# Sliding-window attention on block-diagonal keys with stationary exponentials, its output turned by DMAs, under a new order

## The chip, the cores and the metric

The kernel runs on one core of a Trainium2 chip. The metric is the device time in microseconds of one execution; the kernel before has three such times. A profile is one further execution, recorded instruction by instruction. The engines are named as the profile names them: PE is TensorE (PEld its weight loads), DVE is VectorE, ACT is ScalarE, POOL is GpSimd and SP is the engine that mostly issues DMAs.

## What is computed

The reference normalises x (2048 tokens of width 448), runs a dilated sliding-window attention and a two-layer feed-forward on the normalised rows, and joins them. Cut to what matters:

```
xn = layernorm(x)                               # [2048, 448]
q, k, v = split(xn @ wqkv, heads=16, width=28)
idx = pos[:, None] - 2 * arange(8)              # 8 keys, every second one back
attn = softmax(where(idx >= 0, q . k[idx] / sqrt(28), -1e9))
s = (sum over the 8 of attn * v[idx]) @ wo
h = gelu(xn @ w1 + b1)                          # 448 -> 1792
g = silu(h @ w2 + b2)                           # 1792 -> 448
out = x + s * g
```

The kernel reorders tokens into even ones (first half of 2048 positions) and odd ones, so that the window is eight neighbouring positions. A block of 57 queries then needs 64 neighbouring keys.

## The kernel before

Work is cut into 16 tiles of 128 tokens (four chunks of four tiles) and, for the attention, nine blocks of four strips of 57 (or 56) queries.

**Stages.** `norm` normalises a tile (square root of the variance on ACT in `rstds` for the first four tiles, a power on POOL for the others) and turns it into `xnT`, by PE for the first four tiles and by a transposing DMA (`dma_T`) for the rest. `qk_rows` and `vproj` project to q, k and v; `qk_rows` ends in a transposing DMA that gives `qkT`, with 32 partitions per head in four groups. `values` copies 64 rows of v per strip from `v_tok` to `v`, from SBUF to SBUF on POOL's queue. `ff1`, `ff2_pair` and `ff2` are the feed-forward; `gate` its last function; `final_pair` and `final` multiply with `wo`, and `store` joins and writes out.

**Attention of a block** (`scores`, `values_sum`). The scores are 64 products per block, each with 32 rows of contraction, 64 stationary key columns and 57 query columns, spread over eight corners of the PE array, into four PSUM banks with keys on the partitions. ACT takes the exponential out of each bank (L660), DVE multiplies with the mask (L666). The sums over values are 64 products with v stationary (64 x 32) and the exponentials moving; a column of ones in v gives the softmax sum. Their result has features on the partitions and queries along the row. To divide, DVE transposes each of two banks by 32 x 32 blocks (L692), takes reciprocals (L696), spreads them back by another transpose (L701) and multiplies into `oT` (L706). `move` then repacks the fourth slab of `oT` through DRAM: one store and four loads for every two tiles, on SP.

**Pairs.** Most 448- and 512-column products run as pairs with 64 rows of contraction each, on the upper and the lower half of the array (`pair`). Between the two parts of a pair stands an instruction on POOL or SP that only waits (`told`, L424): PE's second part waits for it, so whatever that queue holds ahead of it delays PE.

**Order.** Each unit of work is a task with its dependencies and buffers. `ORDER` lists every task once, with a letter for its engine (P, V, A, G, S for PE, DVE, ACT, POOL, SP; D for a DMA's landing) and its number by creation. The instructions are emitted exactly in that order, and each engine runs its own in order. Buffers come from small pools (`p_b` has the eight PSUM banks); a task that takes a buffer waits for its last reader.

**Function tables.** ACT holds one table set at a time. Square root, tanh-form gelu, exponential (with tanh) and silu need four different ones; where the set in place is not the one that the next function needs, the built program has a table load ahead of it. Six small tasks made by `table` (L326 to L334) run one function each on a single column (`sink`): gelu, exp, gelu, exp, gelu, silu. In the order before they stand as A54 to A59 in six different places, the first behind the work of the first four tiles and the last near the end:

```
V22 S38 ... S42 D43 A53 G32 ... V61 V64 P9 A62 ... A152 A153 A54 S154
A534 A544 ... A545 A55 V355 ... A784 ... A786 A56 V758 ... A565 A57 ... A840 A58 ... A609 A59
```

Of the kernel before, what the change touches and what calls it, by code (L numbers as in the profile page):

```python
# [8 lines left out]
F32 = mybir.dt.float32  # L9
# [8 lines left out]
D0 V1 G17 S34 D35 A36 D37 V15 P2 V16 V22 S38 D39 V23 V24 G50 V25 V26 V27 P3 S44 D45 V28 V29 V30 G51 D52 V18 V19 P4  # L18
V20 S40 D41 V21 G31 P5 S42 D43 A53 G32 P6 G33 S46 D47 P7 V60 S48 D49 P8 V61 V64 P9 A62 S76 D77 G100 P10 V63 P11 P12
V106 S78 D79 P13 P14 V107 P108 S80 D81 V65 P109 A66 V110 A111 V67 P132 V113 D112 G102 G104 S82 D83 V114 P115 P136  # L20
V117 V68 S86 D87 P116 P133 A118 V69 P190 D119 P137 A70 V71 S88 D89 V120 P134 V121 V72 S90 D91 P122 P123 P135 V73
V191 V124 A74 P138 V75 D125 V126 P149 A139 V127 V140 A143 P128 G150 P129 A148 S141 D142 P151 A152 A153 A54 S154 D155
G178 D179 V130 V144 D131 P321 G174 D175 P326 P163 G327 G322 P323 G164 V96 V94 V95 G168 D169 V97 V92 V145 G99 V200
V204 A325 P328 P165 A166 V201 S202 D203 A330 V205 P341 G342 A324 A329 P336 A167 G337 V84 V85 V93 G98 V192 P343 P338
A339 A340 S206 D207 V105 P331 V193 S194 D195 V196 A344 V197 G332 P156 S198 D199 S274 D275 V309 G157 S272 D273 V298
S278 D279 V304 V305 G186 D187 P333 G188 D189 P158 P316 S146 D147 A335 V311 V312 S276 D277 V307 G317 P346 P318 A160
A159 P227 A345 G347 G184 D185 A319 A334 G228 V308 P348 A350 P229 P526 G527 P546 G252 D253 A320 G547 A349 P528 A529
V300 S161 D162 A530 P536 G537 A231 P548 A550 V310 P538 P516 G517 P215 G294 D295 A230 A549 P518 A519 G216 P222 G223
V103 A520 P217 V219 A539 G180 D181 P224 A540 V301 A225 A226 P521 P531 G522 P523 A525 G532 P533 A524 V218 G170 D171
S220 D221 P208 V302 A535 V303 V299 G306 V101 V359 P541 G209 P210 A211 V351 V363 V364 G542 P543 P621 V360 G172 D173  # L30
S361 D362 A534 A544 V313 V314 V352 G182 D183 P693 A545 A55 V355 V356 S357 D358 G176 D177 G315 V212 V439 A694 V695
A700 A696 V701 V697 G296 D297 G280 D281 A698 G622 S213 D214 P623 V627 G258 D259 P711 A718 A712 V624 A716 P241 S365
D366 V427 V428 A714 V699 A628 P234 V719 G242 P386 V435 G235 V713 S353 D354 V715 S429 D430 S387 G256 D257 P702 P236
V238 A237 P243 V245 P388 V389 A390 P630 G631 G246 D247 A244 G405 D406 S239 D240 A625 V436 V431 P729 S437 D438 G284
D285 P632 A734 V629 V703 V704 V717 V705 V706 A730 A736 P374 V440 S375 A732 V733 S441 D442 S232 D233 G292 D293 G250
D251 V737 P443 G444 V735 V633 G264 D265 G266 D267 G248 D249 P376 V731 P445 A447 A634 V626 G855 V378 P367 V707 A377
P720 V708 V636 A637 G368 V725 V432 A446 V709 V710 G254 D255 V721 P369 A371 S379 A370 D380 V726 V722 V723 V724 P639
S873 D874 V727 V728 P747 A748 A752 G290 D291 G268 D269 G409 D410 S433 D434 S372 D373 V638 A754 V635 G640 P641 V642
P400 G401 P393 V645 A646 V753 A750 P738 P402 S391 D392 V739 G260 D261 P381 A404 G382 V740 V403 S394 P395 A396 V741
V742 V397 G282 D283 P383 A384 G856 G270 D271 V743 V744 G488 D489 V745 V746 P457 S877 D878 G458 S883 D884 A385 P469  # L40
P459 A461 S470 P471 S867 D868 A460 A473 G262 D263 P476 V472 P765 A766 P450 G288 D289 G477 G415 D416 V751 A768 V749
S871 D872 G413 D414 G451 S861 D862 V755 A772 P478 A480 G419 D420 A770 V479 G286 D287 G407 D408 P452 V453 P756 S891
D892 S887 D888 P783 V761 V762 V757 A454 V647 A788 A784 V785 G490 D491 A790 S885 D886 G423 D424 A786 A56 V758 P648
S863 D864 S889 D890 G411 D412 V763 V764 V773 V767 V787 G417 D418 S857 D858 S398 D399 S875 D876 S859 D860 P462 V789
S869 D870 A643 V644 P581 S463 P464 A466 V769 S881 D882 G492 D493 S865 D866 V759 V465 G649 V760 S893 D894 P650 G582
P583 A585 P556 V651 A652 A584 P571 S557 P558 A559 G572 P573 P576 G425 D426 S897 D898 G421 D422 V654 V653 A655 V771
A575 V791 P774 A574 V775 V776 S879 D880 G498 D499 G500 D501 S577 V777 A560 P578 A580 G494 D495 S448 D449 P551 G552
G482 D483 S455 D456 A579 G504 D505 P566 P553 S899 D900 A555 S901 D902 P964 V779 V656 V780 G484 D485 V781 V782 G965
S567 P568 P966 G496 D497 A569 V778 A570 P953 G954 V967 P561 G562 V971 V968 P955 P563 P792 V972 G510 D511 S467 D468
V956 S903 D904 A554 V960 V961 S911 D912 V793 A564 S474 D475 S909 D910 V794 G486 D487 V797 V798 A565 A57 S895 D896  # L50
P801 A804 A802 A806 V795 V796 V803 S969 D970 V805 V807 P657 G658 P819 A822 G512 D513 S905 D906 V799 G502 D503 A820
V800 S913 D914 A808 V809 V957 P659 V663 V660 A664 G481 A824 S907 D908 V823 A826 P810 V815 S919 D920 S962 V811 D963
A661 P666 V816 P837 A842 V812 V817 S915 D916 V813 V818 V814 S973 D974 G667 P668 P975 S958 D959 A844 S923 D924 A838
P986 V843 S987 S921 D922 V662 V672 V665 S927 D928 P591 S929 D930 V669 G976 V825 S925 D926 P988 A840 A58 V827 P977
V989 V990 V982 G592 S931 D932 A673 V993 P593 A595 P586 V821 A594 S587 S991 D992 V674 S917 D918 V983 V978 V979 G506
D507 P596 P588 A590 A589 P828 G597 P598 A599 A600 V829 P616 V833 V830 V831 P611 V834 S612 V835 V836 G617 P618 G514
D515 G508 D509 A619 A620 V832 V845 A670 V994 V839 S984 D985 S933 D934 S941 D942 S935 D936 P1008 G1009 V841 S939 D940
S980 D981 P613 A614 P1010 P601 P606 G607 V1015 G602 A615 P846 V1011 V1012 P603 A604 S1013 D1014 P997 S937 D938 A605
P608 A610 V851 G998 P999 V847 V852 V848 V849 V850 V853 V854 S943 D944 V1000 P675 V1016 S995 D996 A609 A59 P676 V671
V1004 V1005 P687 P688 P679 S1017 D1018 S945 D946 S1006 D1007 V1001 V677 S1002 D1003 P680 A678 P1019 S947 D948 P1024  # L60
P683 P684 S951 D952 S949 D950 P1034 A689 P1029 V681 A682 V1020 V1021 S1022 D1023 P690 P691 V1025 V1026 S1027 D1028
V685 V1035 P1039 V1036 S1037 D1038 A686 V1030 V1031 S1032 D1033 A692 V1040 V1041 S1042 D1043
# [61 lines left out]
def kernel(  # L124
# [31 lines left out]
    for v in range(9):  # L156
        n = NW - 1 if v == 4 else NW
        q = 4 * NW * v - 4 * (v > 4)
        wins = [[q + (2 * w + i) * n for i in range(2)] for w in range(2)]
        VIS.append((q, n, [[(a, a if a in (0, HALF) else a - BACK) for a in ws] for ws in wins]))  # L160
    assert VIS[-1][0] + 4 * VIS[-1][1] == S and VIS[4][2][1][0][0] == HALF
# [32 lines left out]
    v_tok = [sb(f"v_tok{t}", [P, H, 32]) for t in range(9)]  # L194
    v_tok = v_tok[8:] + v_tok[1:8] + v_tok[:8]
    oT = sb("oT", [P, KT, S])
# [4 lines left out]
    m_gen, m_first, m_mid = [sb(n, [P, 2, 4, NW]) for n in ("m_gen", "m_first", "m_mid")]  # L201
    m1 = [sb(f"m1_{i}", [P, 2, NW]) for i in range(3)]
# [9 lines left out]
    p_E = ring("E", 8, [P, 512])  # L212
    p_dt = ring("dt", 2, [P, 512], F32)
    p_rd = ring("rd", 2, [P, H], F32)
# [10 lines left out]
    p_v = ring("v", 6, [P, H, 32])  # L225
# [41 lines left out]
    t_vw = [plan.add("DVE", memset("vector", v[:, :, DH:], 1.0), [t_on]) for v in v_tok[:9]]  # L267
# [213 lines left out]
    v_used = [[] for _ in range(NT + 8)]  # L481

    def vproj(t):
        k0 = t * P

        def part(ps, kt, half, start, stop):
            r = half_rows(half)
            w = w_in[r, kt, 2 * D:] if kt < 3 else w_in3[r, 1, :]
            return nc.tensor.matmul(ps[:, :D], xnT[r, kt, k0:k0 + P], w, start=start, stop=stop)  # L489

        def evac(a, own, i):
            def fn(k):
                copy(k.on, v_tok[t][:, :, :DH], buf(p_b, own, i)[:, :D].rearrange("p (h c) -> p h c", h=H))
            t_vt[t] = plan.add(("ACT", "DVE"), fn, [a] + t_vw + v_used[t], give=((p_b, own, i),))
        return _Job(D, part, [t_xT[t]] + t_w[0] + t_w[1] + t_w[2], evac, (), t_w[3])

    def values(b):

        t_v[b], v_at[b] = [], []
        for i in range(2):  # L500
            first = None
            for w in range(2):
                k0 = VIS[b][2][w][i][1]
# [111 lines left out]
    def moved(v):  # L615
        kept, gone = (0, 1), (2, 3)
        if v:
            kept, gone = gone, kept
        return [x for k, h in zip(kept, gone) for x in ((h, 0, k, 4), (h, 16, h, 3))]

    def move(v, ts):
# [14 lines left out]
        for t in ts:  # L636
            t_oT[t] = t_oT[t] + done
# [286 lines left out]
```

## Time and profile before

| | |
|---|---|
| time, median of three runs | 156.95 us (154.93 to 157.47) |
| span of the profiled execution, first to last instruction | 153.4 us |
| time of the profiled execution around its span | not in the profile; the three runs lie 1.5 to 4.1 us above the span |
| PE busy | 147.6 us (96%) |
| DVE busy | 109.5 us (71%) |
| ACT busy | 87.0 us (57%) |
| POOL busy | 45.5 us (30%) |

Busy time counts instructions in flight. PE's products overlap, so the mean of one product (some 350 ns for 448 columns) is its latency, not what it adds; what it adds is read from the chain of work, where consecutive products of one line are merged into one piece with a start and a length.

### The profile page before, as it was taken

What the parts mean: (1) busy time and instruction counts of PE and PEld (TensorE: products, weight loads), DVE (VectorE), ACT (ScalarE), POOL (GpSimd) and SP (SyncE); (2) the same over time, 40 slices, a digit from 0 to 9 for tenths busy, and PEclk for the clock granted to TensorE, in tenths of its full rate; (3) what the DMA queues carried; (4) which work ended last, traced back from release to release, by engine and by line L of the source; (5) the groups of instructions that cost most, each with busy time, mean ns of one, the idle gap of its engine ahead of it and who ended that gap; (6) DMA issues with size and microseconds to landing.
All of it is one profiled execution on the core that took longest, in us unless ns stands there. A gap on an engine that the chain in (4) does not pass through costs nothing.

```text
span 153.4 us, 5759 instructions
## 1 busy us (share of the span) xinstructions
PE 147.6 (96%) x2404; PEld 79.6 (52%) x2404; DVE 109.5 (71%) x277; ACT 87.0 (57%) x161; POOL 45.5 (30%) x100
## 2 busy tenths in 40 slices
PE   6799999999999999999999999999999999999991
PEld 2344555555565555554556555547655544446551
DVE  5777550465355896899797974788979799898463
ACT  3238687678596634533658727766747356492210
POOL 6832424102592107630468403522200102000000
PEclk9999999999999999999999999999999999999999
DMA  4999966999369953593948700995421012113022
GB/s 152 312 282 306 129 122 137 357 150 279 74 114 145 84 103 84 120 122 63 139 130 167 106 16 21 114 190 41 116 69 47 16 50 56 37 58 118 22 62 60
DMA packets 35442, 18.29 MB, mean 119 GB/s; under 512 B 25643, under 2 KB 34263, under 8 KB 35416
## 3 DMA queue, kind: packets, MB, share of 16 engines
q1 hardware_dynamic: 33208, 14.92, 49.4%
q0 software_dynamic: 2064, 2.88, 8.3%
q8 instruction: 19, 0.31, 1.0%
q10 hardware_dynamic: 144, 0.11, 0.3%
q14 instruction: 7, 0.06, 0.2%
HBM read 7.69 MB, written 2.10 MB: 64 GB/s over the span
## 4 chain that ended last, share of the span: by engine, by line
PE 85%; DMA 7%; DVE 3%; ACT 1%; SPq 1%; issue 1%
PE bank L524 28%; PE bank L550 18%; PE bank L465 11%; PE bank L576 7%; PE bank L489 6%; PE bank L732 5%; PE bank L650 4%; DMA x_sb<-in_A_x_dram 4%; DMA qkT<-qk_tok 4%; PE bank L682 3%; PE bank L747 2%; ACT E L660 1%; SPq L274 1%; DVE E L666 1%; PE bank L389 1%
## 5 line engine op out<-in xcount | busy, mean ns | idle before, releaser
L281 POOL DMA_DIRECT2D v<-v_tok x52 | 27.5, 533 | 73.0 <-PE bank L524 22.7
L528 ACT ACTIVATE h<-bank,b 128x512 bf16<-128x512 f32 x56 | 35.5, 687 | 20.4 <-PE bank L524 20.0
L524 PE MATMUL bank<-xnT,w 64*128 64x512 bf16 x392 | 46.8, 376 | 0.1
L550 PE MATMUL bank<-w,h 64*128 64x448 bf16 x336 | 34.1, 349 | 0.0
L524 PEld LDWEIGHTS <-w 64*128 64x128 bf16 x392 | 21.1, 94 | 19.8 <-SPq L424 0.6
L465 PE MATMUL bank<-w_in,xnT 64*128 64x448 bf16 (+1 forms) x212 | 26.7, 350 | 0.5 <-DMA w_in<-in_A_wqkv_dram 0.3
L550 PEld LDWEIGHTS <-h 64*128 64x128 bf16 x336 | 17.0, 94 | 13.2
L660 ACT ACTIVATE E<-bank 128x456 bf16<-128x456 f32 (+1 forms) x36 | 17.1, 551 | 8.9 <-PE bank L650 8.9
L465 PEld LDWEIGHTS <-xnT 64*128 64x128 bf16 (+1 forms) x212 | 11.0, 94 | 10.2 <-issue 1.4
L340 DVE BATCH_NORM_STATS2 st<-x_sb 128x6 f32<-128x448 bf16 x16 | 9.6, 613 | 8.7 <-DMA x_sb<-in_A_x_dram 8.7
L692 DVE STREAM_TRANSPOSE dt<-bank 128x480 f32<-128x480 f32 (+1 forms) x18 | 11.7, 660 | 4.1 <-PE bank L682 3.8
L592 DVE TENSOR_TENSOR y<-bank,b 128x448 f32<-128x448 f32 x15 | 8.9, 616 | 7.4 <-PE bank L576 4.0
L489 PE MATMUL bank<-w_in,xnT 64*128 64x448 bf16 (+1 forms) x106 | 13.8, 350 | 0.0
L701 DVE STREAM_TRANSPOSE dt<-rd 128x480 f32<-128x480 f32 (+1 forms) x18 | 11.8, 660 | 0.2
L374 DVE TENSOR_SCALAR xn<-x_sb,mv,rstd 128x448 bf16<-128x448 bf16 x16 | 6.1, 395 | 8.2 <-POOL rstd L362 5.4
L706 DVE TENSOR_TENSOR oT<-bank,dt 128x456 bf16<-128x456 f32 (+1 forms) x18 | 11.0, 627 | 0.4
L576 PE MATMUL bank<-w,h 128*128 128x448 bf16 (+2 forms) x70 | 11.3, 315 | 0.0
L666 DVE TENSOR_TENSOR E<-E,m_gen 128x456 bf16<-128x456 bf16 x28 | 10.0, 386 | 1.4 <-ACT E L660 1.4
L604 ACT ACTIVATE t<-y 128x448 f32<-128x448 f32 x12 | 6.9, 577 | 5.1 <-DVE y L592 5.0
L238 ACT CAST qk_tok<-bank 128x448 bf16<-128x448 f32 x11 | 5.8, 534 | 7.1 <-PE bank L465 7.0
L732 PE MATMUL bank<-xn,oT 64*128 64x448 bf16 x42 | 9.4, 349 | 0.0
L732 PE MATMUL bank<-wo,oT 64*128 64x448 bf16 x42 | 9.4, 349 | 0.0
(73 smaller groups left out, 147.5 us busy)
## 6 DMA issues: line engine op xcount, KB each, us to landing
out_dram<-o SPq DMA_DIRECT2D x15, 112.0 KB
w<-in_B_w_dram SPq DMA_DIRECT2D x2, 784.0 KB
w<-in_B_w_dram SPq DMA_DIRECT2D x2, 672.0 KB
x_sb<-in_A_x_dram SPq DMA_DIRECT2D x3, 448.0 KB
v<-v_tok POOLq DMA_DIRECT2D x20, 64.0 KB, 3.0
w_in<-in_A_wqkv_dram SPq DMA_DIRECT2D x3, 336.0 KB
w<-in_B_w_dram SPq DMA_DIRECT2D x4, 112.0 KB
rest<-oT SPq DMA_DIRECT2D x8, 32.0 KB
```

Source lines behind the costliest of these rows:

```text
L281: nc.gpsimd.dma_start(dst(k), src())
L465: return nc.tensor.matmul(ps[:, :D], xnT[r, kt, cs], w, start=start, stop=stop)
L489: return nc.tensor.matmul(ps[:, :D], xnT[r, kt, k0:k0 + P], w, start=start, stop=stop)
L524: return nc.tensor.matmul(ps[:], w1[r, kt, ms], xnT[r, kt, cs], start=start, stop=stop)
L528: nc.scalar.activation(buf(p_h, own, i)[:], buf(p_b, own, i)[:], ACT.Gelu_apprx_tanh, bias=b1[:, mt:mt + 1])
L550: return nc.tensor.matmul(ps[:, :D], buf(*h_at[(c, mt)])[r, j * P:(j + 1) * P], w2[r, mt, :], start=start, stop=stop)
L576: nc.tensor.matmul(ps[:, :n], buf(*h_at[(c, mt)])[:, j * P:(j + 1) * P], w2[:, mt, cs], start=(mt == 0 and not biased), stop=(mt == NMT - 1))
L660: nc.scalar.activation(buf(p_E, k)[:, :n], buf(p_b, a, hl)[:, :n], ACT.Exp, scale=SCALE)
L666: (nc.gpsimd if k.on == "POOL" else nc.vector).tensor_tensor(out=E[:, :n], in0=E[:, :n], in1=m[:, :n], op=ALU.mult)
L692: nc.vector.transpose(buf(p_dt, k)[:, :32 * m], buf(p_b, po, i)[:, :32 * m])
L701: nc.vector.transpose(buf(p_dt, d)[:, :32 * m].rearrange("p (b c) -> p b c", c=32), buf(p_rd, r)[:, :m].unsqueeze(2).to_broadcast((P, m, 32)))
L732: return nc.tensor.matmul(ps[:, :D], oT[r, kt, t * P:(t + 1) * P], wo[v][r, kt, :], start=start, stop=stop)
```

## The change

The attention is rewritten and everything is put in a new order.

- **Keys.** A new task `keys` copies 64 keys of each strip twice into `kb`, once multiplied by a column that keeps the even 32-partition groups and zeroes the odd ones, once the other way round (`plane`). One head of each pair thus occupies its own 64 of 128 stationary columns. This runs on ACT (21 instructions, 13 of them with 1024 elements per partition and 8 with 512) or on DVE (one).
- **Scores.** 32 products per block instead of 64, each 64 rows by 128 stationary columns by 57 moving columns; two halves of a block (`p`), two banks each.
- **Values.** The exponentials become the stationary side (64 x 128) and v moves, two strips at once, 58 columns: 32 products per block instead of 64. The result has queries on the partitions and features along the row, so that the division is one reciprocal of 8 columns (L718) and one multiplication (L723) per bank, of which there are 36; the transposes are gone.
- **v** goes through DRAM: `vproj` stores each tile to `v_rows`, `values` loads strips from there. Both are DMAs of POOL.
- **Output** goes by rows to `o_rows` in DRAM (36 stores, SP) and comes back by 16 transposing DMAs (`turn`, SP), into `xnT` for the first eight tiles and `oT_late` for the rest. `move` and its 40 DMAs go. `load_wo` takes 2 DMAs instead of 8 for each of the two packings.
- **Masks.** 25 of the 36 mask multiplications stay on DVE, 11 go to POOL.
- **Order.** A new `ORDER`. Its first three lines hold the small square root on ACT and all six `table` tasks (A51 to A57), ahead of the first square root of real data (A60):

```
D0 V1 A34 D35 G17 S32 D33 V15 P2 V16 V18 V22 V23 A51 V24 S36 D37 V25 V19 A52 G48 V20 V21 P3 A53 V26 G49 D50 A54 S42
D43 A55 A56 P4 S38 D39 A57 G98 P5 S40 D41 S44 D45 P6 S46 D47 P7 G100 P8 V58 P9 V59 S74 D75 V62 A60 P10 S76 D77 P11 V61
```

The core of the diff:

```diff
-    def scores_of(b):
-            for i in range(2):
-                for g in range(G):
-                    for hl in range(4):
-                        for w in range(2):
-                            r = slice(32 * hl, 32 * hl + 32)
-                            nc.tensor.matmul(banks[hl][NK * w:NK * w + NK, c0:c0 + nq], qkT[r, 1, g, k0:k0 + NK],
-                                             qkT[r, 0, g, q0:q0 + nq], start=True, stop=True)
+    def keys(b):
+                    src = strided(qkT[:, 1, :, k0:k0 + NK], n, step)
+                    dst = buf(p_kb, first or k)[:, j:j + n, :, e, :]
+                    if k.on == "ACT":
+                        nc.scalar.mul(dst, src, plane[:, e:e + 1])
+                    else:
+                        nc.vector.tensor_scalar(dst, src, plane[:, e:e + 1], None, op0=ALU.mult)
+    def scores(b, p):
+            for g in range(G):
+                for i in range(2):
+                    for r in range(2):
+                        h = slice(64 * r, 64 * r + 64)
+                        nc.tensor.matmul(buf(p_b, k, r)[:, c0:c0 + nq], buf(p_kb, t_kb[b][0])[h, 2 * p + i, g].rearrange("p e k -> p (e k)"),
+                                         qkT[h, 0, g, q0:q0 + nq], start=True, stop=True)
-                            nc.tensor.matmul(banks[w][32 * g:32 * g + 32, c0:c0 + nq], v[r, 4 * g + hl, :],
-                                             E[r, c1:c1 + nq], start=True, stop=True)
-            nc.vector.transpose(buf(p_dt, k)[:, :32 * m], buf(p_b, po, i)[:, :32 * m])
-            nc.vector.reciprocal(buf(p_rd, k)[:, :m], ...)
-            nc.vector.transpose(buf(p_dt, d)[:, :32 * m]..., buf(p_rd, r)[:, :m].unsqueeze(2).to_broadcast((P, m, 32)))
-            nc.vector.tensor_tensor(out=oT[:, :, q0:q0 + 2 * nq], ...)
+                        nc.tensor.matmul(buf(p_b, k, e)[:, 2 * DV * x:2 * DV * x + 2 * DV], buf(p_E, exps[r])[h, 2 * nq * g:2 * nq * g + P],
+                                         v[h, 2 * p:2 * p + 2, x, :DV], start=True, stop=True)
+                nc.vector.reciprocal(buf(p_rd, k)[rows], sums(k, e)[:, :, 0, DH])
+                nc.vector.tensor_tensor(out=o, in0=sums(k, e)[:, :, :, :DH], in1=..., op=ALU.mult)
+                nc.sync.dma_start(o_rows[n + i * nq:n + i * nq + nq, :], buf(p_a, own)[i * nq:i * nq + nq, i, :])
+    def turn(t, v):
+        t_oT[t] = [dma_T(oT(slice(0, P), slice(0, KT), t * P, t * P + P), lambda: o_rows[t * P:t * P + P, PAD - PAD * v:PAD - PAD * v + 512],
+                         t_oT[t], None)]
```

More of the change, by code (lines that the diff above doesn't have):

```diff
@@ L23 @@
[L23 to L32, printed above, removed]
@@ L193, with oT @@
     qkT = sb("qkT", [P, 2, G, S])
-    v_tok = [sb(f"v_tok{t}", [P, H, 32]) for t in range(9)]
-    v_tok = v_tok[8:] + v_tok[1:8] + v_tok[:8]
-    oT = sb("oT", [P, KT, S])
+    v_tok = [sb(f"v_tok{i}", [P, H, 32]) for i in range(4)]
+    v_rows = dram.tile([S, H * 32], BF16, name="v_rows")
+    PAD = 64
+    o_rows = dram.tile([S, D + 2 * PAD], BF16, name="o_rows")
+    oT_late = sb("oT", [P, KT, HALF])
+    def oT(r, kt, c0, c1):
+        if c1 <= HALF:
+            return xnT[r, kt, c0:c1]
+        assert c0 >= HALF
+        return oT_late[r, kt, c0 - HALF:c1 - HALF]
+    plane = sb("plane", [P, 2], F32)
     ident = sb("ident", [P, P])
@@ L480 @@
     t_vt = {}
-    v_used = [[] for _ in range(NT + 8)]
     def vproj(t):
@@ L491, in evac @@
         def evac(a, own, i):
+            b = v_tok[t % len(v_tok)]
             def fn(k):
-                copy(k.on, v_tok[t][:, :, :DH], buf(p_b, own, i)[:, :D].rearrange("p (h c) -> p h c", h=H))
-            t_vt[t] = plan.add(("ACT", "DVE"), fn, [a] + t_vw + v_used[t], give=((p_b, own, i),))
+                copy(k.on, b[:, :, :DH].rearrange("p (e x) c -> p e x c", e=2),
+                     buf(p_b, own, i)[:, :D].rearrange("p (x e c) -> p e x c", e=2, c=DH))
+            d = plan.add(("ACT", "DVE"), fn, [a] + t_vw + [t_vt[u] for u in (t - len(v_tok),) if u >= 0], give=((p_b, own, i),))
@@ L657, in weights_of, with f2 @@
         exps, masked = [], []
-        for hl in range(4):
-            def f2(k, hl=hl):
-                nc.scalar.activation(buf(p_E, k)[:, :n], buf(p_b, a, hl)[:, :n], ACT.Exp, scale=SCALE)
-            e = plan.add("ACT", f2, [a], take=(p_E,), give=((p_b, a, hl),))
+        for r in range(2):
+            def f2(k, r=r):
+                nc.scalar.activation(buf(p_E, k)[:, :n], buf(p_b, a, r)[:, :n], ACT.Exp, scale=SCALE)
+            e = plan.add("ACT", f2, [a, t_pad[0]], take=(p_E,), give=((p_b, a, r),))
@@ L792 @@
     t_mask = []
-    for m, w1_, n, first in ((m_gen, m1[0], NW, None), (m_first, m1[1], NW, 0), (m_mid, m1[2], NW - 1, 1)):
+    for m, w1_, n, first in ((m_gen, m1[0], NW, False), (m_first, m1[1], NW, True)):
         def fn(_, s=w1_, n=n, first=first):
@@ L796, in fn @@
             for w in range(2):
-                for i, c in ((0, 1), (1, 1)) if w == first else ((0, 2),):
-                    back = BACK if w == first and not i else 0
+                for i, c in ((0, 1), (1, 1)) if first else ((0, 2),):
+                    back = BACK if first and not i else 0
                     a = s[NK * w:NK * w + NK, i:i + c, :n]
```

313 lines of the change are left out of this document (155 added, 158 removed).

## The prediction

> **What bounds the kernel now.** I read the page first, then the list of PE's waits, then the chain of work that ended last, then ACT's and SP's rows.
>
> ```profile
> span 153.4 us, 5759 instructions
> PE 147.6 (96%) x2404; PEld 79.6 (52%) x2404; DVE 109.5 (71%) x277; ACT 87.0 (57%) x161; POOL 45.5 (30%) x100
> ...
> PE 85%; DMA 7%; DVE 3%; ACT 1%; SPq 1%; issue 1%
> ```
>
> ```profile
> PE bank L253 <- DVE eps_t L245: 1.5, 1, 1.5
> PE bank L465 <- DMA w_in<-in_A_wqkv_dram: 0.3, 1, 0.3
> PE bank L389 <- DVE xn L374: 0.3, 1, 0.3
> PE bank L465 <- DVE xnT L240: 0.2, 1, 0.2
> PE bank L650 <- DMA qkT<-qk_tok: 0.2, 1, 0.2
> ```
>
> PE is the bound. These five lines are the whole list of its waits, and but for the last they lie in the first ten microseconds. The chain says the same: one PE piece after another from 9.92 us to 150.10, and where it leaves PE (the transposing DMA at 62.41) PE was fed from elsewhere, for it waited only 0.2 us in the end.
>
> ```profile
> 2.19 5.84 DMA x_sb<-in_A_x_dram
> ...
> 9.26 0.18 DVE rstd L355
> ...
> 9.46 0.41 DVE xn L374
> ...
> 9.92 0.45 PE bank L389 x4
> ...
> 36.70 3.02 PE bank L524 x28
> ...
> 45.84 2.75 PE bank L550 x28
> 48.59 0.63 PE bank L650 x64
> ...
> 51.79 0.61 PE bank L682 x64
> ...
> 62.41 5.50 DMA qkT<-qk_tok
> ...
> 149.40 0.70 PE bank L576 x14
> ...
> 150.73 0.22 DVE o L763
> ```
>
> From here come PE's prices: a half-array product of 512 columns adds 3.02/28 = 0.108 us, one of 448 columns 2.75/28 = 0.098, a block's attention 0.63 + 0.61 = 1.24 us for 128 products, 9.7 ns each. A full-array product of 112 columns adds 0.70/14 = 50 ns. DVE (71%) and ACT (57%) are covered by PE on the average, so work taken from DVE alone gains nothing, and work given to ACT or SP costs only where it holds PE up. The sum runs against 153.4 us of span; the median, 156.95, lies 3.6 above it, the fastest run, 154.93, 1.5.
>
> **The change part by part.** *The head.* ACT's first rows, and two later ones, give the price of a table load:
>
> ```profile
> 1.21 1.28 ACT L321 ACT_TABLE_LOAD   x1 [1.21 <-PEq L908]
> 2.51 0.20 ACT L321 ACTIVATE sd<-eps_t 128x1 f32<-128x1 f32 x1
> ...
> 8.94 0.29 ACT L352 ACTIVATE sd<-mv,eps_t 128x1 f32<-128x1 f32 x1 [0.51 <-DVE mv L344]
> ...
> 13.41 0.97 ACT L238 CAST qk_tok<-bank 128x448 bf16<-128x448 f32 x2 [0.74 <-PE bank L465]
> 14.39 1.28 ACT L327 ACT_TABLE_LOAD   x1
> 15.68 0.20 ACT L327 ACTIVATE sink<-eps_t 128x1 f32<-128x1 f32 x1
> ```
>
> A load takes 1.28 us, and its function starts 0.01 us behind it; together 1.49. In the new order all six `table` tasks follow the first load, ahead of any square root of real data, each with a load of its own since neighbours differ; then the square root needs its set again. So: 2.71 (first load and function) + 6 x 1.49 = 11.65, + 1.28 = 12.93, + 0.29 for `sd` = 13.22, + 0.18 `rstd` + 0.41 `xn` and their gaps: PE's first transposes start near 13.9 us instead of 5.34.
>
> ```profile
> 1.52 3.55 PE L253 MATMUL bank<-h 128*128 128x512 bf16 x13 [1.52 <-DVE eps_t L245]
> 5.34 0.45 PE L389 MATMUL bank<-ident,xn 128*128 128x128 bf16 x4 [0.28 <-DVE xn L374]
> ```
>
> ```profile
> 5.30:9.90 4.60, 3.93 (x24) 1.84 (x24) 2.96 (x12) 1.24 (x4) 3.35 (x14) 1.00 1.04 323
> ```
>
> That is +8.5. Some is given back, since by 13.9 all inputs have landed: in the window from 5.30 to 9.90 us (columns: length, then busy time of PE, PEld, DVE, ACT, POOL) PE was busy 3.93 of 4.60 us, 0.7 lost at least, and its small groups there end one by one, so that I take 1.2: +7.3 (bounds +4 and +7.8). Behind this PE has stood idle some 9 us. The first row has 13 warm-up products, eight of 512 and five of 128 columns: 4736 columns in 3.55 us, 0.75 ns per column, against 0.70 us/(14 x 112) = 0.45 later. So a restarted PE may be slow for some 4 us again: 0 to +1.8, I take +1.5, the nearest case being this kernel's own start.
>
> *The attention's products.* 1152 products go, 9 x 1.24 = 11.2 us. 576 come, 64 rows by 128 stationary columns by 57 or 58 moving. The trace has none. From below each costs what one of the old ones costs, some 10 ns, since both halves of the array can work at once: 5.8 us, -5.4. From above it costs a full-array product of 112 columns, 50 ns: 28.8, +17.6. By the row of 448 columns in half arrays, 98 x 57/448 = 12.5 ns; with 128 weight columns changed for each product more than that. I take 20 ns: 11.5, so 0.
>
> *DVE's work.* These groups shrink or go:
>
> ```profile
> L692 DVE STREAM_TRANSPOSE dt<-bank 128x480 f32<-128x480 f32 (+1 forms) x18 | 11.7, 660 | 4.1 <-PE bank L682 3.8
> ...
> L701 DVE STREAM_TRANSPOSE dt<-rd 128x480 f32<-128x480 f32 (+1 forms) x18 | 11.8, 660 | 0.2
> ...
> L706 DVE TENSOR_TENSOR oT<-bank,dt 128x456 bf16<-128x456 f32 (+1 forms) x18 | 11.0, 627 | 0.4
> ```
>
> 34.5 us and the reciprocals go; 36 multiplications by at most 0.627 (22.6) and 36 reciprocals of 8 columns come, 11 masks move to POOL. DVE gets lighter, but PE did not wait for it: 0.
>
> *ACT in the body.* The keys add 21 copies, their lengths estimated from these rows: 448 elements in 0.54, 256 in 0.37, 0.85 ns per element, so 1024 take 1.02 us and 512 take 0.59: 13 x 1.02 + 8 x 0.59 = 18 us. And with the `table` tasks gone from their places, the functions themselves call the loads: the built order has 14 in the body, where there were six. The gelus of FF1 are interleaved with exponentials.
>
> ```profile
> 18.27 1.85 ACT L528 ACTIVATE h<-bank,b 128x512 bf16<-128x512 f32 x3
> ...
> 46.02 1.88 ACT L660 ACTIVATE E<-bank 128x456 bf16<-128x456 f32 x4 [0.27 <-PE bank L650]
> ```
>
> ```profile
> L327 ACT ACT_TABLE_LOAD x6 | 7.7, 1283 | 0.1
> ...
> L604 ACT ACTIVATE t<-y 128x448 f32<-128x448 f32 x12 | 6.9, 577 | 5.1 <-DVE y L592 5.0
> L238 ACT CAST v_tok<-bank 128x448 bf16<-128x448 f32 x13 | 6.6, 541 | 2.2 <-PE bank L489 2.2
> ...
> L238 ACT COPY xnT<-bank 128x256 bf16<-128x256 bf16 x2 | 0.7, 372 | 1.9 <-PE bank L389 1.9
> ```
>
> A gelu adds 1.85/3 = 0.62, an exponential 1.88/4 = 0.47. Two stretches of the new order alternate fast. The first, around the first attention blocks, has three loads: ACT 3.9 + one gelu 0.6 + eight exponentials 3.8 + two tanh 1.0 + three casts 1.4 + three keys 3.0 = 13.7; PE beside it 126 products of 448 columns, 12.4, + 111 of the attention, 2.2 = 14.6. It nearly balances, but the keys on ACT wait for the transposing DMA of q and k, 5.50 us behind a cast that ACT itself does: what is queued behind the waiting copy (exponentials, gelus, bank evictions) starves PE. +3 (0 to +6). The second, in the second half of FF1, has eight loads: ACT 8 x 1.28 = 10.2 + fourteen gelus 8.7 + eight exponentials 3.8 + two tanh 1.0 + a cast 0.5 + two keys 2.0 = 26.2; PE 84 x 0.108 = 9.1 + 92 x 0.098 = 9.0 + 112 x 0.02 = 2.2, together 20.3. ACT sets the pace there: +6 (0 if banks and order let PE run ahead, +10 if each load is exposed).
>
> A rule of the Trainium skill speaks to this: its page ScalarE: Activation LUTs, section What ACT_TABLE_LOAD costs, says that beside the load of some 1.28 us a switch costs a drain of about 1.38 us, 2.66 in all. The trace has the 1.28 but shows no drain: the load at 14.39 follows the end of the cast and the function follows the load. The last rival below follows it.
>
> *SP.*
>
> ```profile
> 62.41 1.30 SPq L287 DMA_TRANSPOSE qkT<-qk_tok  x1
> ...
> 68.94 0.48 SPq L627 DMA_DIRECT2D rest<-oT  x1
> ```
>
> 16 more transposing DMAs at 1.30 and 36 stores at 0.48 make 38 us of issuing; `move` gives back eight stores and 32 loads, 0.48 each from above, 19, less if a load is shorter: +19 to +23 us on the queue that also issues the transposes of q, k and `xnT` and carries some of the pair's `told` waits (15 on SP now, 11 before). A store waits for DVE's division and a transpose for its store, so a late block delays what stands behind. In 150 us of span there is room on the average: +1 (0 to +4). v's way through DRAM adds a hop on POOL, ahead of its use by a tile's work or more: 0. At the end, `oT_late` is turned over 10 us of PE work ahead of the last products, so the tail from 149.40 on stays 3.3 us.
>
> Sum: 153.4 + 7.3 + 1.5 + 0 + 6 + 3 + 1 = 172.2 us of span; with the 1.5 that the fastest run lies above it, 173.7, I say 173.5.
>
> **The rivals.**
>
> *Only the head shows.* PE's order has slack in front of the exponentials, banks hold eight results, and ACT is 57% busy now; then the loads in the body hide. 153.4 + 7.3 + 1.5 + 0 to 1 = 162.2 to 163.2, a time of 164 to 166. For it: ACT's idle gaps before (1 to 3 us ahead of many gelus). Against: 26.2 us of ACT work beside 20.3 of PE.
>
> *SP's queue and the keys decide.* In four places the keys on ACT come right behind the issue of the transposing DMA that they need. If each holds ACT 4.5 us (5.50 less one piece of work), and PE has no cover, that is 18 instead of the 3 + 1 counted, less some 2 that falls together with loads: +12, a time near 186.
>
> *Not slower.* The half-array products overlap fully, at 12.5 ns or less: 576 x 12.5 = 7.2, -4.0 us; and a freed DVE and fewer hops give another 3 by letting PE's groups close up in the head (its bound +4 instead of +7.3), no slow restart, no stall in the body: 153.4 - 4.0 + 4 = 153.4, a time of 154.9 to 157.0. It decides only if all eight loads of the second stretch hide, that is if PE finds at least 6 us of other work there.
>
> *Each switch costs twice.* If ACT also emptied itself around a load and lost as much again, 1.28 us, each of the 18 loads counted above would cost it: 7 x 1.28 = +9 in the head, 11 x 1.28 = +14 in the two stretches: 173.5 + 23 = 196.5. Against it stand the rows at 14.39 and 15.68 without a gap. This is the mechanism of the Trainium skill's page ScalarE: Activation LUTs, section What ACT_TABLE_LOAD costs; by its 1.38 us of drain it would be about 198.
>
> **How the numbers follow.** Forecast 0.57, only the head 0.21, SP and keys 0.17, not slower 0.03, twice the price 0.02. The range goes from 163, the head alone, to 187, the keys' case: what lies outside is the last two and some edges of the others, about 2 in 10 together. About 2% can be told from no change, so the limits are 153.8 and 160.1. Slower 0.95; within 2% 0.04, the third rival and the lower edge of the first; faster 0.01.
>
> **What would show it.** Right: seven more table loads ahead of the first square root of data, PE's first transposes near 13.9 us; in the second half of FF1 a list of PE waits on gelus and exponentials of some 6 us; ACT near 125 us busy. The attention's pieces in the chain show 0.6 us per 32 products if 20 ns is right, 1.6 if it is 50. Wrong: PE at 95% behind the head (first rival); waits of ACT on qkT's DMA of over 4 us in four places (second); PE's first transposes far from 13.9; a gap of over a microsecond around each load (last).

## The result and the profile after

The changed kernel takes 202.56 us in the median of four runs (200.68 to 202.68), the kernel before 157.0 (154.93 to 157.47): a ratio of 1.292 (95% interval 1.281 to 1.303). It is slower, as forecast, but by 45.6 us instead of 16.5, and 15.6 us above the top of the range. Single executions of a kernel can come out some per cent longer at a lower granted clock; the ratios, here and below, leave those out, the medians do not.

The page of the kernel after (busy times; then, in 40 slices of 5 us, PE's busy share and its granted clock in tenths):

```profile
span 200.9 us, 4637 instructions
PE 156.7 (78%) x1828; PEld 94.2 (47%) x1828; DVE 102.2 (51%) x264; ACT 123.5 (61%) x193; POOL 50.5 (25%) x94
...
PE   6119999982499959919989688059596899999993
...
PEclk9999999997579999985999999859999999999999
```

PE was busy 96% of the span before, now 78% of a longer one. The missing work is not spread out: there are holes near 5, 45, 90 and 125 us, and behind the last three the granted clock falls as well. ACT's 123.5 us of work is what was forecast ("near 125"), so the amount of work was right and the waiting was not.

The first five rows of PE's list of waits, kernel after (engine and line, what ended the wait; us in total, times, the longest):

```profile
PE bank L677 <- ACT h L556: 8.5, 2, 7.3
PE bank L403 <- DVE xn L388: 8.4, 1, 8.4
PE bank L552 <- POOLq L438: 5.0, 2, 4.8
PE bank L479 <- ACT h L556: 4.1, 2, 3.0
PE bank L677 <- ACT kb L660: 4.1, 1, 4.1
```

Before, the whole list came to 2.5 us. Here 8.4 are the head, as forecast. The other rows name a gelu (L556), a hop (L438) and a key copy (L660): they say who let PE go, not what had held that engine. For that one reads the same list of ACT:

```profile
ACT kb L660 <- DMA qkT<-qk_pair: 20.6, 3, 10.6
ACT kb L660 <- DMA qkT<-qk_tok: 14.6, 4, 4.6
...
ACT kb L660 <- issue: 2.7, 1, 2.7
```

ACT stands 38 us, at eight places, in front of a key copy. At seven of them (35.2 us) a transposing DMA ends the wait; for the eighth (2.7 us, "issue") the profile names nothing. ACT runs its list in order, so gelus that free PSUM banks, casts of v and exponentials stand behind it. ACT's rows, kernel after (start, length, line and what it does; in brackets the idle time before, and what ended it):

```profile
10.30 1.28 ACT L341 ACT_TABLE_LOAD   x1
11.59 0.20 ACT L341 ACTIVATE sink<-eps_t 128x1 f32<-128x1 f32 x1
11.81 1.28 ACT L366 ACT_TABLE_LOAD   x1
13.11 0.29 ACT L366 ACTIVATE sd<-mv,eps_t 128x1 f32<-128x1 f32 x1
...
34.03 0.73 ACT L660 ACTIVATE kb<-qkT,plane 128x512 bf16<-128x512 bf16 x1
...
51.63 1.15 ACT L660 ACTIVATE kb<-qkT,plane 128x1024 bf16<-128x1024 bf16 x1 [10.59 <-DMA qkT<-qk_pair]
52.68 3.56 ACT L556 ACTIVATE h<-bank,b 128x512 bf16<-128x512 f32 x6
...
63.03 0.72 ACT L660 ACTIVATE kb<-qkT,plane 128x512 bf16<-128x512 bf16 x1 [2.68 <-DMA qkT<-qk_tok]
...
82.56 1.15 ACT L660 ACTIVATE kb<-qkT,plane 128x1024 bf16<-128x1024 bf16 x1 [2.72 <-issue]
88.27 2.19 ACT L660 ACTIVATE kb<-qkT,plane 128x1024 bf16<-128x1024 bf16 x2 [4.56 <-DMA qkT<-qk_tok]
...
129.52 1.15 ACT L660 ACTIVATE kb<-qkT,plane 128x1024 bf16<-128x1024 bf16 x1 [5.04 <-DMA qkT<-qk_pair]
130.69 1.28 ACT L556 ACT_TABLE_LOAD   x1
131.98 1.26 ACT L556 ACTIVATE h<-bank,b 128x512 bf16<-128x512 f32 x2
133.27 1.28 ACT L683 ACT_TABLE_LOAD   x1
```

The first rows are the head: the last of the extra loads, then the square root's own, and `sd` at 13.11. The key copy at 51.63 ends at 52.78, and the gelus behind it start at 52.68. Now SP's rows, kernel after, where the transposing DMAs are issued (the length is that of issuing):

```profile
52.80 1.23 SPq L301 DMA_TRANSPOSE qkT<-qk_tok  x1
...
78.90 6.18 SPq L301 DMA_TRANSPOSE qkT<-qk_tok  x2
```

The first is issued 0.02 us after that key copy ends. The second row is two DMAs that need some 2.5 us to issue and take 6.18 together: the copy at 82.56 ends at 83.71 in the middle of it, and the next copy waits 4.56 us for the DMA issued then. Copy and DMA take turns: each DMA into `qkT` seems to wait for the copy before it, and each copy for every DMA issued ahead of it, whether or not it reads what that DMA writes. The copy at 63.03 (A653) bears this out: it reads the same keys as the one at 34.03 (A651) and multiplies them with the other column of `plane`. These keys had thus landed 29 us before, and still it waits 2.68 us for a DMA into `qkT`. The experiments test this.

PE's rows, kernel after:

```profile
14.09 0.61 PE L403 MATMUL bank<-ident,xn 128*128 128x128 bf16 x4 [8.45 <-DVE xn L388]
14.87 0.93 PE L479 MATMUL bank<-w_in,xnT 128*128 128x448 bf16 x2 [0.17 <-DVE xnT L252]
...
20.67 0.54 PE L479 MATMUL bank<-w_in,xnT 128*128 128x448 bf16 x2
...
53.40 2.23 PE L479 MATMUL bank<-w_in,xnT 64*128 64x448 bf16 x8 [2.95 <-ACT h L556]
...
89.48 0.57 PE L677 MATMUL bank<-qkT,kb 64*128 64x57 bf16 x16 [4.06 <-ACT kb L660]
89.86 1.68 PE L479 MATMUL bank<-w_in,xnT 64*128 64x448 bf16 x8
...
109.38 0.92 PE L479 MATMUL bank<-w_in,xnT 64*128 64x448 bf16 x8
```

Eight products of one shape take 0.92 us in a stretch without waits, 1.68 behind a wait of 4.06 us and 2.23 behind the stall near 50 us. A stall is thus paid twice, as the wait and as slow products after it. In the head the pair at 14.87 takes 0.93 us, a pair of the same shape at 20.67 takes 0.54.

### The profile page after: what moved, and what is told of

The parts are those of the page before. It is cut to its first block, busy times and chain, and to the rows that moved or that the text cites. A ratio compares the mean times of both kernels' runs of the same rounds, so it can differ in the third digit from the quotient of the medians.

```text
span 200.9 us, 4637 instructions
## 1 busy us (share of the span) xinstructions
PE 156.7 (78%) x1828; PEld 94.2 (47%) x1828; DVE 102.2 (51%) x264; ACT 123.5 (61%) x193; POOL 50.5 (25%) x94
## 5 line engine op out<-in xcount | busy, mean ns | idle before, releaser
L660 ACT ACTIVATE kb<-qkT,plane 128x1024 bf16<-128x1024 bf16 (+1 forms) x21 | 20.4, 986 | 38.0 <-DMA qkT<-qk_pair 20.6
L479 PE MATMUL bank<-w_in,xnT 64*128 64x448 bf16 (+1 forms) x212 | 35.4, 409 | 6.3 <-ACT h L556 4.1
L556 ACT ACTIVATE h<-bank,b 128x512 bf16<-128x512 f32 x56 | 35.0, 688 | 7.6 <-PE bank L552 7.4
L723 DVE TENSOR_TENSOR a<-bank,rd 114x448 bf16<-114x448 f32 (+1 forms) x36 | 22.5, 624 | 1.2
L295 POOL DMA_DIRECT2D v_rows<-v_tok x16 | 9.1, 571 | 48.4 <-ACT v_tok L250 23.9
L295 POOL DMA_DIRECT2D v<-v_rows x22 | 13.6, 623 | 27.1 <-PE bank L708 11.8
L677 PE MATMUL bank<-qkT,kb 64*128 64x57 bf16 (+1 forms) x288 | 8.9, 193 | 14.4 <-ACT h L556 8.5
L693 DVE TENSOR_TENSOR E<-E,m_gen 128x456 bf16<-128x456 bf16 (+1 forms) x24 | 8.9, 395 | 15.0 <-ACT E L683 14.9
L677 PEld LDWEIGHTS <-kb 64*128 64x128 bf16 x288 | 8.1, 98 | 17.9 <-issue 11.6
L502 PE MATMUL bank<-w_in,xnT 64*128 64x448 bf16 (+1 forms) x106 | 16.4, 373 | 0.0
L693 POOL TENSOR_TENSOR E<-E,m_gen 128x456 bf16<-128x456 bf16 x8 | 8.8, 1106 | 26.3 <-ACT E L683 26.3
L718 DVE RECIPROCAL rd<-bank 114x8 f32<-114x8 f32 (+1 forms) x36 | 7.2, 200 | 12.9 <-PE bank L708 12.9
```

The costliest lines, as they stand in the source:

```text
L295: nc.gpsimd.dma_start(dst(k), src())
L479: return nc.tensor.matmul(ps[:, :D], xnT[r, kt, cs], w, start=start, stop=stop)
L556: nc.scalar.activation(buf(p_h, own, i)[:], buf(p_b, own, i)[:], ACT.Gelu_apprx_tanh, bias=b1[:, mt:mt + 1])
L660: nc.scalar.mul(dst, src, plane[:, e:e + 1])
L677: nc.tensor.matmul(buf(p_b, k, r)[:, c0:c0 + nq], buf(p_kb, t_kb[b][0])[h, 2 * p + i, g].rearrange("p e k -> p (e k)"), qkT[h, 0, g, q0:q0 ...
L693: (nc.gpsimd if k.on == "POOL" else nc.vector).tensor_tensor(out=E, in0=E, in1=m, op=ALU.mult)
```

## The experiments

Theory: the keys' waits set the time (38 us on ACT), the head adds 9 to 10 us and the loads in the body 6 or so. Rivals: the order by itself (the bulk loads on SP ahead of the transposing DMAs, or PE's own sequence); the keys' work on ACT rather than their wait.

**One part at a time.** Six kernels, one run each with a profile, and all beside the kernel before: 156.6 us (one run) beside the first four, 157.07 (median of seven, 154.02 to 158.99) beside the other two.

`e1_static`: keys and scores read a block that lies still (`w1`) instead of `qkT`; the attention's dependence on the transposing DMAs is left out, all instructions stay.

```diff
-                    src = strided(qkT[:, 1, :, k0:k0 + NK], n, step)
+                    src = strided(w1[:, :, k0 % 1024:k0 % 1024 + NK], n, step)
-                                         qkT[h, 0, g, q0:q0 + nq], start=True, stop=True)
+                                         w1[h, g, q0 % 1024:q0 % 1024 + nq], start=True, stop=True)
```

> Keys and scores read a block of w1, long loaded, in place of the transposed q and k (which are still made); every instruction and its length stays, only the wait for the transposing DMAs goes. This leaves the true attention out. Theory A, ACT is held in its own order by key copies that wait for the transposing DMAs (38 us of waiting at L660), and PE starves behind it: the span falls by 25 to 35 us, to 166 to 176 us. Theory B, the table loads in the body set ACT's pace: it falls by under 8 us, to 193 or more. Theory C, SP's queue as such (it stays as full as it is): under 8 us too.

182.29 us, span 180.6: 20.3 less. The waits of the key copies are gone. What PE still waits for (its list, `e1_static`):

```profile
PE bank L403 <- DVE xn L388: 8.6, 1, 8.6
PE bank L552 <- POOLq L438: 5.9, 1, 5.9
PE bank L479 <- SPq L438: 2.7, 4, 1.7
```

The wait for a hop on POOL, which begins near 44 us in the changed kernel, stands without any key wait: it belongs to the order.

`e2_oneset`: FF1's gelus become exponentials, so that no load stands between them (another function is computed).

```diff
-    ... ACT.Gelu_apprx_tanh ...     # ff1's eviction, L556
+    ... ACT.Exp ...
```

> FF1's evictions use the exponential in place of the gelu, so exponential, tanh and these share one set: of 14 loads in the body two stay. Theory A: the 12 loads are 15.4 us of ACT's time, but ACT is idle far longer behind its waits, so the span falls by 3 to 9 us, to 192 to 198 us. Theory B: it falls by 15 to 30 us, to 171 to 186 us.

192.19, span 190.5: 10.4 less, with 12 loads fewer (22 before, 10 now): 0.87 us for each.

`e3_head`: the six `table` tasks (A52 to A57) leave the first three lines and stand ahead of functions that need their set anyway.

```diff
-... A51 ... A52 G48 ... A53 ... A54 S42 D43 A55 A56 P4 ... A57 G98 ... A60
+... A51 ... G48 ... S42 D43 P4 ... G98 ... A60 ... P300 A52 A297 ...
```

> The six table tasks stand one by one ahead of functions that load that set anyway (first gelu, first exponential, and so on), so seven loads of the head go and none comes. All theories: PE's first transposes near 5.3 us instead of 14.1 and the span 7 to 9 us shorter, 192 to 194 us, if what follows merely moves up; less, 196 to 199, if the transposing DMAs or weight loads, which do not start earlier, take it back.

192.56, span 190.8: 10.1 less.

`e4_keys_dve`: the 21 key copies move from ACT to DVE, at the same places of the list.

```diff
-... A650 ... A651 ... A652 ...
+... V650 ... V651 ... V652 ...
```

> All 21 key copies of ACT go to DVE at the same places of the order. Theory A: the wait moves to DVE, whose queue holds evictions and masks too; PE starves less by what ACT's gelus no longer wait, 8 to 20 us, to 181 to 193 us. Theory B: ACT has 20 us less work, the stretch of loads gets 2 us of it back: 197 to 199 us.

201.84, span 200.1: 0.8 less, no difference. DVE's list of waits in `e4_keys_dve`:

```profile
DVE kb L662 <- DMA qkT<-qk_tok: 14.9, 5, 5.9
...
DVE kb L662 <- DMA qkT<-qk_pair: 6.4, 3, 3.1
```

Taking 20.4 us of copying off ACT gained nothing; the wait moved along with the copies. `e1` is the other side of this: there all the copying stays on ACT, only its waits go, and the span is 20.3 us shorter. So the keys' work on ACT is not the cost.

`e5_three_together`: `e1`, `e2` and `e3` in one.

> The edits of the first three experiments together: keys and scores on w1 instead of the transposed q and k, exponential in place of the gelu, table tasks out of the head. This leaves the true attention and the gelu out. If the three causes are separate, the span is 200.9 - 20.3 - 10.4 - 10.1 = 160 us (157 to 163). If the keys' waits and the loads hide in one another, 164 to 170. What is left above 150 (before, less 3 us that the attention's products save) is a fourth cause, and I expect it in the stall near 44 us, where PE waits for a hop on POOL behind the loads of x.

167.08, span 165.4. The three together take 35.5 us of span, against 40.8 for their sum. The exponentials save less here than in `e2`: the small gelus of the `table` tasks now stand in the body and call loads of their own, so that 7 loads go against `e3`, not 12 (8 are left, 7 in the kernel before). At 0.87 us each the five account for 4.4 of the 5.3 us that are missing. Ten of the 45.6 us remain (twelve against the three fastest runs of the kernel before beside it, 154.02 to 155.74), with no key wait, one load more than before and no delayed head.

`e6_w2_behind`: SP's loads of `w` (FF2) and POOL's loads of `wo` go behind the transposing DMA of q and k that ACT's first long wait is for (S230, tile 3; in the changed kernel it is issued at 40.01 us and takes 8.31 us to issue).

```diff
-S262 D263 ... S260 D261 ... G268 D269 ... G266 D267 ... S230 D231
+... S230 D231 S262 D263 S260 D261 G268 D269 G266 D267
```

> Only the order of SP's and POOL's loads is changed: the two loads of w2 and those of wo move behind the transposing DMA of q and k of tiles 6 and 7, which in the changed kernel took 8.31 us to issue behind them. If SP's queue of bulk loads makes the first long wait (10.6 us of ACT at L660, PE idle 4.8 and 3.0 us), the span falls by 4 to 8 us, to 193 to 197. If the loads of x, or the keys as such, make it, by under 2 us.

205.22, span 203.5: 2.6 more, a miss. The first key wait did shrink, from 10.59 to 6.30 us, but PE stood just there for the hop on POOL (6.7 us instead of 4.8): that wait was beside another one. The time does not hang on these loads; those of x, on the same queue, stayed where they were and were not tried.

**Why a copy waits for DMAs it does not need.** A key copy reads two to four strips of 64 keys whose starts are 57 apart, as one access; neighbouring strips overlap by seven keys. Every second strip has a start 114 apart, and no overlap. `e8_key_halves` copies them so, in two instructions; order and everything else stay.

```diff
-                    src = strided(qkT[:, 1, :, k0:k0 + NK], n, step)
-                    dst = buf(p_kb, first or k)[:, j:j + n, :, e, :]
+                    for x in range(min(n, 2)):
+                        src = strided(qkT[:, 1, :, k0 + x * step:k0 + x * step + NK], n // 2, 2 * step)
+                        dst = buf(p_kb, first or k)[:, j + x:j + n:2, :, e, :]
```

> The changed kernel in its own order, with each key copy that reads two or four overlapping strips of 64 keys (57 apart) split into two copies of every second strip, whose reads do not overlap. In the built program a copy with overlapping strips waits for every transposing DMA of q and k issued ahead of it and each later transposing DMA waits for it, needed or not; a split copy waits only for the tiles that it reads. ACT has 21 instructions more (some 4 us). Theory A1, the needless waits make most of the loss at the keys: ACT's wait at L660 falls from 38 us to under 15 and the span by 12 to 20 us, to 181 to 189. Theory A2, the needed landing (5 us behind the issue) makes it: the wait stays above 30 us and the span within 4 us of 200.9.

188.55 (186.66 to 188.85), ratio 1.2177 [1.208, 1.2275]: 14.0 us by the medians, 0.074 or 11.7 us by the ratios. ACT's whole list of key waits in `e8_key_halves`, and below it SP's row that answers to the one at 78.90:

```profile
ACT kb L661 <- DMA qkT<-qk_pair: 16.7, 2, 10.5
```

```profile
77.19 2.64 SPq L301 DMA_TRANSPOSE qkT<-qk_tok  x2
```

The waits fall from 38.0 to 16.7 us (under 15 were expected), and the pair of DMAs goes out in 2.64 instead of 6.18, no longer held by a copy. More than half of the waiting was needless: the program as built orders an access with overlapping strips against everything around it in `qkT`. The longest wait was not: the 10.59 us at 51.63 are still 10.5 here, so that copy waits for a landing that it needs. Its block reads keys up to token 455, and tile 3, which starts at 384, comes with the DMA that `e6` brought forward without a gain.

`e7_own_order` and `e9_halves_own_order` test the same under another order: all tasks of the changed kernel, listed anew with FF, projections and `table` tasks where the kernel before has them, and all key copies and masks on DVE (the list is long and not shown). `e9` adds the two copies of `e8`.

> All tasks of the changed kernel under an order of my own: the shared tasks in the places that they have in the kernel before, the attention put in with at least some 5 us between a transposing DMA and its key copy, key copies on DVE, table tasks ahead of the functions, masks on DVE. If the order alone makes the loss, the span is that of before less the products' gain, 150 to 156 us, and the time within 2% of before or better. If the new form itself costs (36 stores and 16 transposes on SP, the round trip through DRAM, 14 ns products), 162 to 175 us.

174.87 (174.49 to 177.36), ratio 1.129 [1.101, 1.157]; DVE's waits for keys in `e7_own_order`:

```profile
DVE kb L662 <- DMA qkT<-qk_pair: 16.4, 4, 5.3
DVE kb L662 <- DMA qkT<-qk_tok: 10.2, 3, 4.5
```

> My own order as run before (span 172.4 us), with the same split of the key copies (on DVE, one on top of 0.3 us each). A1: DVE's wait for the transposing DMAs (26.6 us at the key copies) falls below 10 us, and the span to 156 to 164. A2: the wait stays and the span at 170 to 174.

160.86 (160.0 to 164.25), ratio 1.0392 [1.0295, 1.049]: again 14.0 us less by the medians, 0.090 or 14.1 us by the ratios. DVE's waits for keys in `e9_halves_own_order`, 4.4 us where 26.6 were:

```profile
DVE kb L663 <- DMA qkT<-qk_tok: 4.0, 2, 3.1
...
DVE kb L663 <- DMA qkT<-qk_pair: 0.4, 1, 0.4
```

**The account in the change's own order.** `e13_halves_head` is `e8` and `e3` together; `e14_halves_head_oneset` adds `e2`'s exponentials.

> The changed kernel's own order with split key copies and the table tasks moved from the head to the functions. If the two add up, the span is 185.0 - 10.1 = 175 us (173 to 177). If the earlier head only runs into DMAs that are no earlier, 178 or more.

179.07 (177.46 to 182.15), ratio 1.1301 [1.1193, 1.1409]: 9.5 us less than `e8` by the medians, 13.8 by the ratios; `e3` alone gave 10.1.

> The same with the exponential in place of the gelu, which leaves the gelu out and takes 12 loads out of the body. If the loads are a cause of their own, as my prediction's +6 and +3 said, the span falls by 8 to 12 us against the run before it, to 163 to 167. If they cost so much in the second experiment only because they stood behind late keys, by 0 to 4 us. What is left above 150 then is the order's.

172.01 (171.04 to 173.99), ratio 1.0909 [1.0819, 1.0998]: 7.1 less than `e13`, 6.2 by the ratios. As in `e5`, only 7 loads go (15 to 8) and not the 12 of the expectation: 0.9 to 1.0 us for each, in line with the 0.87 of `e2`. What PE still waits for, first in its list in `e14_halves_head_oneset`; then POOL's row there; then PE's:

```profile
PE bank L552 <- POOLq L438: 8.6, 2, 6.8
```

```profile
40.89 0.30 POOL L375 TENSOR_SCALAR sd<-mv,eps_t 128x4 f32<-128x4 f32 x1 [10.42 <-DVE mv L358]
```

```profile
41.30 1.46 PE L552 MATMUL bank<-xnT,w 64*128 64x512 bf16 x6 [6.81 <-POOLq L438]
44.15 2.23 PE L479 MATMUL bank<-w_in,xnT 64*128 64x448 bf16 x8 [1.39 <-ACT h L556]
```

POOL stands 10.42 us in front of the variances of later x tiles (L375), and the hop that PE waits for is behind it; then PE runs slowly. The changed kernel shows the same wait, and DVE's list there what is behind it; last, POOL's wait in the kernel before:

```profile
POOL sd L375 <- DVE mv L358: 8.4, 1, 8.4
```

```profile
DVE st L354 <- DMA x_sb<-in_A_x_dram: 8.6, 3, 5.9
```

```profile
POOL sd L361 <- DVE mv L344: 1.9, 1, 1.9
```

The variances wait for DVE's statistics, and those for the landing of x. DVE waits about as long for x in the kernel before (8.7 us), but there POOL stands only 1.9 us and PE waits for no hop: the new order puts POOL's variances, and the hop behind them, too early in POOL's list for when x lands. This is read from the rows and was not tried by itself.

**How good can the new attention be?** `e10_order_rebuilt` lists `e9`'s tasks in a new order that allows for later landings of the DMAs; `e11_hops_on_pool` is `e9` with eleven hops of `pair` from SP to POOL; `e12_rebuilt_pool` is a rebuilt order with hops on POOL.

```diff
-... S363 ... S347 ... S370 ... S444 ... S437 ... S513 ... S533 ... S523 ... S995 ... S543 ... S568
+... G363 ... G347 ... G370 ... G444 ... G437 ... G513 ... G533 ... G523 ... G995 ... G543 ... G568
```

> Split key copies on DVE and an order built anew with 6.3 us between the issue of a transposing DMA and its key copy, and the split copies' lengths. If order and needless waits are all that was wrong, the span is 150 to 156 us and the time within 2% of before or below it. If the new form needs more than before (SP's 52 stores and transposes more, slow PE starts behind stalls), 157 to 165.

166.37 (165.63 to 167.23), ratio 1.0779 [1.0689, 1.0869]: a miss, worse than `e9`.

> The split key copies in my own order as before, with the 11 hops between the parts of pairs that stood on SP now on POOL, at the same places. In that run PE waited 5.9 us for hops on SP, behind stores and transposing DMAs that wait for DVE and for their landing. If SP's new queue of 52 stores and transposes is what the form still costs, these waits go and the span falls by 3 to 7 us, to about 152 to 156 us and a time within 2% of before. If the hops merely wait on POOL instead (behind v's stores), by under 2 us.

159.76 (158.76 to 163.93), ratio 1.0323 [1.0195, 1.0451]: the best version of the new form, 1.1 us under `e9`, inside their intervals. It is slower than the kernel before, but its interval reaches to both sides of 2%.

> An order built anew with all hops on POOL, 6.3 us between a transposing DMA's issue and its key copy, and the attention 1 us behind its places in the kernel before: a second try at the same repair. Span 152 to 157 us if the hops were the rest, 159 to 164 if the order built anew loses as the former one did (163.9).

163.43 (161.28 to 166.67), ratio 1.0463 [1.0353, 1.0573]: a miss as well. No version beat the kernel before.

The chain of `e11_hops_on_pool` shows the attention's pieces where PE runs at full speed:

```profile
90.02 0.22 PE bank L678 x16
99.61 0.22 PE bank L709 x16
```

## Why the prediction was wrong

*The head: right.* 8.8 us (7.3 and 1.5 for a slow restart) against 10.1 in `e3` and 9.5 in `e13` (13.8 by the ratios, so perhaps a little small). PE's first transposes were to start near 13.9 and start at 14.09; the pair of 0.93 us at 14.87 is the slow restart, which lasts to about 20 us, longer than the 4 taken.

*The products: a term mis-sized, without harm.* 0.22/16 = 14 ns each, not 20. A block's 64 take 0.88 us where 128 took 1.24, about 3.2 us less for nine blocks instead of 0. They lie nearest to the row of 448 columns scaled down (12.5 ns).

*DVE: right.* 102.2 us busy, no bound. *SP: not contradicted.* The hops moved off SP in `e11` are worth 1.1 us, within their intervals, where +1 was forecast; what the new stores and transposing DMAs cost by themselves was not tried.

*The loads in the body: right in size.* The +6 was for eight loads, and three more were within the +3. `e2` measured 10.4 us for 12 loads and `e14` 6.2 to 7.1 for 7, so 0.87 to 1.0 us each, 7 to 8 for the eight. The sign given for it came out smaller: in the second half of FF1 (133 to 160 us) PE's waits on gelus and exponentials come to 4.0 us, not 6. The rival that each switch costs twice is out: at 130.69 the load follows the copy and the gelu follows the load by 0.01 us, as in the head. The drain of about 1.38 us that the Trainium skill's page ScalarE: Activation LUTs, section What ACT_TABLE_LOAD costs, adds to a load is in no row here.

*The keys: the step that failed.* It was written as "+3 (0 to +6)" in the first stretch, and the rival had "four places" at 4.5 us. Both took a copy to wait for the landing of its own tiles. It waits at eight places, 38 us in all, longest 10.59. Split copies take 11.7 to 14.1 us off the time in two orders: the needless waits. Needed landings, 16.7 us of ACT's waiting in `e8` and the longest wait among them, cost something more: 5 us by `e14` (172.0) against `e5` (167.1), but `e5` is one run, and each taken against the kernel before in its own group leaves 2. So 2 to 5 us. The mechanism named for the rival, ACT in order with gelus behind a waiting copy, was the right one; that the built program ties the copy to all of `qkT` around it was not seen, though the changed access pattern was in the diff. And each stall's slow products were counted in the head alone.

*The order: missing from the sum.* `e14` lies 14.3 us over the kernel before. The needed landings (2 to 5) and SP (1) less the products (3) leave some 11 to 14 to the order, by subtraction; `e5`, without key waits and delayed head and with one load more than before, is 10 to 12 us over. Under another order, with the key copies and masks on DVE, most of that goes: `e11` is at +3.2% (2.0 to 4.5). Which part of the order costs how much was not tried. The prediction costed an order only at the places where ACT's and PE's sums met, and never asked what a hop on POOL stands behind.

Together, in the order of the runs: 14.0 for needless key waits, 9.5 for the head, 7.1 for loads, and the 14.3 that `e14` keeps; by the ratios 11.7, 13.8, 6.2 and 14.3. That this comes to the 45.6 us proves nothing, since each kernel is the one before it with one part more. The first three are measured by one change each; how the 14.3 divides into landings, SP, products and order is argued. The rivals "only the head shows" and "not slower" are out with the loads and the keys; "SP's queue and the keys decide" named the right engine and the right wait at half its number of places.

## What to carry to other kernels

When a change replaces exact reads by one strided access, look whether its pieces overlap: the program may then order it against every writer of that buffer, and on an engine that runs in order all that stands behind it waits too. Before costing a new order, list each waiting instruction that stands ahead of a hop or an eviction on its engine, and price a stall of PE at its length plus the slow products after it. Moving the waiting instruction to another engine moves the wait (20.4 us of copies moved, 0.8 gained); removing what it waits for removes it.

## What the runs showed of the hardware

PE's slow restart comes in the middle of a kernel as well: eight products at 1.68 to 2.23 us instead of 0.92, and in the windows of the kernel after (length, busy time of PE, PEld, DVE, ACT, POOL, then the granted clock):

```profile
14.00:44.00 30.00, 29.25 (x239) 13.88 (x239) 13.12 (x44) 17.97 (x33) 9.96 (x17) 1.00 0.65 134
44.00:66.00 22.00, 13.97 (x105) 7.01 (x105) 10.02 (x33) 10.85 (x18) 3.93 (x6) 0.77 0.81 154
```

The stretch with the stall near 45 us has 0.77. The one before it shows 1.00, although its first pairs took 0.93 us instead of 0.54: here the clock row missed a slow start, and the products' own lengths are the safer sign. The Trainium skill's page TensorE: Matmul & The Clock Gate, section Part 1: The HAM clock gate, says that an idle window of some 3.4 us halves the clock and a busy one of that length restores it. The rows agree that a wait of 4 to 8 us is followed by products at about half speed; the slow stretch in the head lasted over 5 us (14.09 to 20), longer than that.

A key copy of 1024 elements is far shorter on DVE than on ACT. The groups of the kernel after:

```profile
L660 ACT ACTIVATE kb<-qkT,plane 128x1024 bf16<-128x1024 bf16 x13 | 14.6, 1146 | 30.3 <-DMA qkT<-qk_pair 15.6 <-DMA qkT<-qk_tok 12.0 <-issue 2.7
...
L662 DVE TENSOR_SCALAR kb<-qkT,plane 128x1024 bf16<-128x1024 bf16 x1 | 0.5, 484 | 0.0
```

1146 ns against 484. The versions `e7` and `e9` to `e12` have all key copies on DVE; no run compares the two places with the needless waits gone.
